# An attention and feed-forward kernel whose instruction order is written by a list scheduler in the kernel file, with a first chunk of 512 tokens

## The chip, the core and the metric

The kernel runs on one core of a Trainium2 chip. The metric is device time in microseconds (us) of one execution, as the median of several. A core has five engines, each with its own instruction queue: TensorE (PE in the profile; its weight loads are shown as PEld), VectorE (DVE), ScalarE (ACT), GpSimd (POOL) and SyncE (SP), which here issues all transfers. PSUM is the memory into which TensorE writes, in eight banks of 512 float32 columns on 128 partitions; everything else lies in SBUF.

## The reference

Inputs are q, k and v of shape 8 x 8 x 576 x 64 (batch, heads, positions, head width), and two weight matrices, 512 x 2048 and 2048 x 512. Two attentions are added and a feed-forward layer follows:

```python
    q_d = q.reshape(B, H, Sd, factor, D).mean(axis=3)     # factor 4: 144 pooled positions; k_d, v_d alike
    out_up = np.repeat(sm_attn(q_d, k_d, v_d), factor, axis=2)
    mask = np.abs(pos[:, None] - pos[None, :]) < factor   # local attention over 7 neighbours
    scores = np.where(mask, scale * np.matmul(q, k.transpose(0, 1, 3, 2)), -1000000000.0)
    ...
    x = (out_up + out_local).transpose(0, 2, 1, 3).reshape(B * S, H * D)    # 4608 tokens x 512
    h = x @ w_in                                          # 2048 wide
    g = np.where(h >= 1, h, np.where(h <= -1, 0.0, (h + 1) ** 2 / 4))
    return g @ w_out
```

## The kernel before, in words

**Attention** goes by pairs of heads: a batch has four pairs, so there are 32 pairs, n = 0 to 31. The function `attention(n, ...)` (L154) is a generator cut into pieces by `yield`. A pair loads q and k (transposed, 288 KB each), windows of v (320 KB) and pooled v (288 KB). DVE sums q and k in groups of four (L161, L165). PE computes local scores of ten windows of 64 positions into `sl_ps` (L186) and pooled scores into `sp_ps` (L200; a third of them goes to free columns of `sl_ps`). DVE and ACT, with help of POOL, make the two softmaxes (L218 to L260). For the pairs of batch 0 (`early`) the band mask is added by PE, with two matmuls of the identity with the band (L174), and POOL normalises (L254); for all others DVE adds the band (L221), POOL subtracts the maximum (L225), and DVE normalises. PE transposes both (`tl_ps` L272, `tp_ps` L284), ACT copies them out of PSUM, PE multiplies with v (`pl_ps` L306, `pp_ps` L318), and DVE adds the two (L329). The result x is split into a rounded part `xh` (ACT, L336) and a remainder `xl` (POOL, L337), in a ring buffer of two batches.

**Weights** come as 64-bit floating-point words, which the kernel converts itself, in 32 tiles (`convert_weights`, L354; tile f of w_in and of w_out for f = 0 to 15): two ACT operations on the halves of the words (L360, L362), a shift and an addition on DVE (L365, L366), then the split into a rounded part (ACT, L368) and a remainder (DVE, L369). All converted tiles stay in SBUF.

**The feed-forward layer** goes by chunks of 384 tokens, twelve chunks, and for each by 16 steps f of 128 hidden columns. `mm1` (L439) does twelve matmuls (four blocks of inputs, times hi x hi, lo x hi and hi x lo) into `h_ps`; then come ACT (L458, L459), DVE (L460), ACT for the rounded part `gh` (L463) and POOL for the remainder `gl` (L464). `mm2` (L467) does nine matmuls (three groups of 128 tokens, three products) and accumulates over the 16 steps in three banks `o_ps`; after the last step ACT copies them and SP stores them. Chunk 0 needs all tiles of weights for the first time, so the 32 conversions lie ahead of and in it, together with the attention of batch 1 (pairs 4 to 7).

**The order.** Up to the end of pair 3 and through chunk 0, the order in which work is emitted is written out by hand in two lists, `BEFORE_STEPS` and `FIRST_STEPS` (L76, L80): `q` and `v` are loads, `w` loads of weights, `a0` the next piece of pair 0, `c` a conversion, `s` a step of mm1, `m` one of mm2. From chunk 1 on a loop does at each step some pieces of attention, an `mm1`, and the `mm2` of an earlier step (L490). This order gives the priorities; the framework's scheduler makes each engine's instruction order from them, and `mm1`'s elementwise part is raised in priority (L455).

**PSUM.** In the first stage (pairs 0 to 3) there are `ps_a2` (2 banks), `ps_a1` (1 bank), `ps_b2` (2 buffers of 2 banks) and `ps_b1` (1 bank), used in rotation. Afterwards the b pools give way to `ps_h` (2 banks) and `ps_o` (3 banks), and all attention goes through `ps_a2` and `ps_a1`.

## Time and profile before

| what | value |
|---|---|
| median of 3 runs | 1008.16 us (1005.01 to 1008.43) |
| the profiled execution | 1007.57 us |
| its span, first to last instruction | 1005.8 us |
| instructions | 18468 |
| granted TensorE clock, mean | 0.98 of full speed |
| busy: PE / ACT / DVE / POOL | 969.0 / 488.6 / 396.3 / 351.2 us |

The span is a little shorter than the execution's time, since that also holds what lies before the first and after the last instruction. The profile's views that are used below are: the page's list of engines and its row of 40 equal slices (each digit is the busy share in tenths); the busy times of each engine in chosen windows; the timeline, with an instruction's start, its duration and, in brackets, how long its engine had been idle before it and what it waited for; and groups of equal instructions with their count, their total busy time and the mean duration of one in nanoseconds, and behind a bar the idle time ahead of them. An instruction's duration on PE is longer than the distance between two starts, because matmuls overlap; so PE's rates are read from starts.

### The profile page before, as it was taken

How to read it: one execution, taken by the hardware profiler on the slowest of the kernel's cores; microseconds unless marked ns; L12 is line 12 of the kernel's file. 1: busy time of each engine (PE TensorE's matmuls, PEld its weight loads, DVE VectorE, ACT ScalarE, POOL GpSimd, SP SyncE). 2: the span in 40 equal slices, each digit the busy share in tenths (PEclk: the TensorE clock that was granted, in tenths of full speed). 3: DMA queues.
4: the chain of work that ended last, by engine and by line, in shares of the span. 5: the costliest groups of instructions: out<-in, count | busy, mean ns of one | idle time of the engine just before them, and what ended most of it. 6: DMA issues, size and time to landing. Idle time of an engine off the chain costs nothing.

```text
span 1005.8 us, 18468 instructions
## 1 busy us (share of the span) xinstructions
PE 969.0 (96%) x7612; PEld 845.3 (84%) x7612; DVE 396.3 (39%) x700; ACT 488.6 (49%) x1063; POOL 351.2 (35%) x327
## 2 busy tenths in 40 slices
PE   5698999999999999999999999999999999999997
PEld 4476779998888888998888888999888888899996
DVE  6879991124434442113444434112434444111111
ACT  5778754335445444334445444434444454433433
POOL 2532443223434433223433334222334344222222
PEclk8689999999999999999999999999999999999999
DMA  9685111002112221002222112001212210000000
GB/s 304 228 294 172 50 50 57 1 12 92 50 50 94 61 74 57 1 1 66 64 74 71 59 50 75 33 1 41 63 50 74 91 63 15 32 1 1 32 1 33
DMA packets 26533, 66.24 MB, mean 66 GB/s; under 512 B 3152, under 2 KB 3152, under 8 KB 26448
## 3 DMA queue, kind: packets, MB, share of 16 engines
q1 hardware_dynamic: 26448, 65.06, 20.0%
q8 instruction: 60, 0.98, 0.4%
q14 instruction: 25, 0.20, 0.1%
HBM read 55.61 MB, written 9.44 MB: 65 GB/s over the span
## 4 chain that ended last, share of the span: by engine, by line
PE 79%; DVE 9%; issue 5%; POOL 3%; ACT 3%; DMA 1%; SPq 0%; POOLq 0%; DVEq 0%; ACTq 0%
PE h_ps L447 34%; PE o_ps L478 33%; PE tp_ps L284 2%; PE pl_ps L306 2%; PE sl_ps L186 2%; PE tl_ps L272 2%; DVE m L366 2%; PE pp_ps L318 2%; POOL gl L464 1%; PE sp_ps L200 1%; DVE m L365 1%; DVE w_o L369 1%; DMA raw_i<-w_in 1%; DVE w_i L369 1%; DVE u L460 1%
## 5 line engine op out<-in xcount | busy, mean ns | idle before, releaser
L447 PE MATMUL h_ps<-xh,w_i 128*128 128x384 f32 x1536 | 406.3, 344 | 0.6 <-DVE u L460 0.6
L464 POOL TENSOR_TENSOR gl<-u,gh 128x384 fp32r<-128x384 f32 x192 | 198.2, 1032 | 539.2 <-ACT gh L463 403.2
L478 PE MATMUL o_ps<-w_o,gh 128*128 128x512 f32 x1152 | 357.6, 391 | 1.0 <-ACT gh L463 1.0
L447 PEld LDWEIGHTS h_ps<-xh,w_i 128*128 128x128 f32 x1536 | 277.3, 188 | 20.9 <-issue 10.1
L460 DVE SCALAR_TENSOR_TENSOR u<-h_ps,u 128x384 f32<-128x384 f32 x192 | 106.8, 556 | 450.3 <-ACT u L459 424.3
L447 PE MATMUL h_ps<-xl,w_i 128*128 128x384 f32 x768 | 261.8, 341 | 0.0
L478 PEld LDWEIGHTS o_ps<-w_o,gh 128*128 128x128 f32 x1152 | 213.7, 188 | 33.4 <-ACT gh L463 1.7
L478 PE MATMUL o_ps<-w_o,gl 128*128 128x512 f32 x576 | 226.2, 393 | 3.8 <-POOL gl L464 3.6
L458 ACT ACTIVATE u<-h_ps 128x384 f32<-128x384 f32 x192 | 94.6, 492 | 272.8 <-PE h_ps L447 272.8
L463 ACT CAST gh<-u 128x384 fp32r<-128x384 f32 x192 | 98.6, 514 | 112.8 <-DVE u L460 112.8
L447 PEld LDWEIGHTS h_ps<-xl,w_i 128*128 128x128 f32 x768 | 144.4, 188 | 0.7 <-issue 0.4
L478 PEld LDWEIGHTS o_ps<-w_o,gl 128*128 128x128 f32 x576 | 108.1, 188 | 30.4 <-POOL gl L464 7.3
L459 ACT ACTIVATE u<-u 128x384 f32<-128x384 f32 x192 | 100.4, 523 | 5.0
L225 POOL TENSOR_TENSOR sl<-sl,mxl 128x640 f32<-128x640 f32 x28 | 35.8, 1280 | 52.7 <-DVE mxl L224 52.7
L264 POOL TENSOR_TENSOR vh<-vp_sb 72x512 f32<-72x512 f32 x32 | 42.3, 1322 | 29.7 <-DMA vp_sb<-vp 15.5
L337 POOL TENSOR_TENSOR xl<-x,xh 128x576 fp32r<-128x576 f32 x32 | 46.2, 1445 | 14.5 <-ACT xh L336 14.5
L329 DVE TENSOR_TENSOR x<-pl_ps,xd 128x576 f32<-128x576 f32 x32 | 24.2, 755 | 56.0 <-ACT xd L327 56.0
L221 DVE TENSOR_TENSOR sl<-sl_ps,band_sb 128x640 f32<-128x640 f32 x28 | 23.1, 823 | 40.8 <-PE sl_ps L200 40.8
L249 DVE TENSOR_REDUCE sp_ps<-sl 128x10 f32<-128x640 f32 x32 | 26.4, 825 | 28.2 <-ACT sp L240 28.2
L306 PEld LDWEIGHTS pl_ps<-al,v_sb 64*64 64x64 f32 x1280 | 23.8, 145 | 14.1 <-issue 9.9
L272 PE MATMUL tl_ps<-ident,sl 128*128 128x128 f32 x160 | 25.7, 296 | 9.8 <-POOL sl L254 5.3
L272 PEld LDWEIGHTS tl_ps<-ident,sl 128*128 128x128 f32 x160 | 20.0, 151 | 16.3 <-POOL sl L254 6.2
(67 smaller groups left out, 756.2 us busy)
## 6 DMA issues: line engine op xcount, KB each, us to landing
v_sb<-vw SPq DMA_DIRECT2D x32, 320.0 KB
vp_sb<-vp SPq DMA_DIRECT2D x32, 288.0 KB
out<-osb SPq DMA_DIRECT2D x36, 256.0 KB
raw_i<-w_in SPq DMA_DIRECT2D x16, 512.0 KB
raw_o<-w_out SPq DMA_DIRECT2D x16, 512.0 KB
q_sb<-qT SPq DMA_DIRECT2D x28, 288.0 KB
k_sb<-kT SPq DMA_DIRECT2D x28, 288.0 KB
first_i<-qT SPq DMA_DIRECT2D x4, 288.0 KB
```

The lines of the kernel that those rows point to most:

```text
L225: nc.gpsimd.tensor_tensor(slf, slf, ml_n, op=ALU.subtract)
L264: nc.gpsimd.tensor_tensor(vh, vpt[:, :, 0:2, :], vpt[:, :, 2:4, :], op=ALU.add)
L272: nc.tensor.transpose(tl_v[:, g * P : (g + 1) * P], sl[:, g].rearrange("p r c -> p (r c)"), ident)
L306: nc.tensor.matmul(pl_v[hs, o : o + OUT_LEN[i]], v[rs, 2 * g + h, :], al[rs, g, c0 : c0 + OUT_LEN[i]], start=True, stop=True,)
L337: nc.gpsimd.tensor_tensor(xl[:, p, r0 : r0 + S], x, xh[:, p, r0 : r0 + S], op=ALU.subtract)
L447: nc.tensor.matmul(h[:, :TCH], wi[:, wt, cc * P : (cc + 1) * P], xt[:, cc, ts], start=(n == 0), stop=(n == 3 * NCC - 1),)
L458: nc.scalar.activation(u, h[:, :TCH], AF.Relu, bias=0.5, scale=0.5)
L459: nc.scalar.activation(u, u, AF.Square)
L460: nc.vector.scalar_tensor_tensor(u, h[:, :TCH], 1.0, u, op0=ALU.max, op1=ALU.min)
L463: nc.scalar.copy(gh, u)
L464: nc.gpsimd.tensor_tensor(gl, u, gh, op=ALU.subtract)
L478: nc.tensor.matmul(o, gt[:, ts], wo[:, wt, :], start=f == 0 and n == 0, stop=f == NFC - 1 and n == 2)
```

## The change

The two hand-written lists, the loop over steps and the PSUM pools go. In their place every operation is described to a class `Plan`: its engine, its expected duration, the operations it needs, the buffers it uses, and a key, the time at which it is due. `Plan.run` walks through time: for every engine it looks for the operations whose inputs and buffers are there, takes the one with the lowest key among those that can start within 0.15 us of the first, and of all engines the one that starts first; it marks its buffers and its end, with 0.10 us from one engine to another and 0.25 us from PE, and with operations on DVE that are marked `shared` prolonged by 0.7 of their overlap with POOL. `Plan.emit` then emits the operations in that order, under a manual schedule, so that each engine's instruction order is the planned one; the framework still puts in the semaphores.

Beside that:

- Chunks are 512, 256 and then ten times 384 tokens. Chunk 0 accumulates in four banks (4 to 7), chunk 1 in two.
- PSUM is one tile of eight banks, given out by the plan. Batch 0 uses four pairs of banks for `sl`, `sp`, `tl`, `tp` and `pl`; batch 1 uses banks 0 and 1 for all of these, chunk 0 and 1 use 2 and 3 for `h`; from batch 2 on `sp` has bank 2 and shares the second bank of `sl`, as before. `pp` goes into free columns of `pl`'s banks.
- `early`, the band mask by PE and the subtraction on DVE, now holds for eight pairs instead of four. Normalising (L254) is on DVE for all pairs. Maxima and sums of the softmaxes are in SBUF instead of PSUM, `qd` has two buffers and `gl` two instead of three.
- Weight tiles, the first batch's q, k, v and the scratch of pairs 1 and 3 share 32 slots: weights from f = 4 on wait for slots that batch 0 has held.
- Loads are issued in the planned order on SP: q and k of the first four pairs, then their v, then weights, and later pairs 30 us ahead of their due time.

```diff
-TCH = 384
-NCH = NT // TCH
-NTT = TCH // P
 RING = 2 * S
...
+CHUNKS = [(0, 512), (512, 256)] + [(t, 384) for t in range(768, NT, 384)]
+NCH = len(CHUNKS)
...
-BEFORE_STEPS = """
-    q0 v a0 a0 w q1 a0 a0 a1 w a1 q2 a0 a1 c a0 a1 a2 w c a0 a2 q3 a1 c a2 a0 a1 a2 a0 c
-    a3 a1 a3 a2 c a3 a0 a1 a2 a3 c a1 a2 a3 a1 a2 a3 a2 a3 w a2 a3 a3 w a3
...
-FIRST_STEPS = """
...
+class Plan:
+
+
+    LATENCY = 0.10
+    PE_LATENCY = 0.25
+    DMA_RATE = 370e3
+    DMA_LATENCY = 2.0
+    WINDOW = 0.15
+    BACKLOG = 4.0
+
...
+    def run(self):
...
+        while len(done) < total:
+            best = None
+            for e in engines:
+                cands = []
+                for o in ready[e]:
+                    t = based.get(o.n)
+                    if t is None:
+                        t = based[o.n] = settle(o)
+                    ok = True
+                    for b in o.bufs:
+                        if b.units is None:
+                            got = pick(b)
+                            if got is None:
+                                ok = False
+                                break
+                            t = max(t, got[0] + self.LATENCY)
+                    if ok:
+                        if e == "SP":
+                            t = max(t, dma_free - self.BACKLOG)
+                        cands.append((max(t, free[e]), o))
+                if not cands:
+                    continue
+                t0 = min(c[0] for c in cands)
+                t, o = min((c for c in cands if c[0] <= t0 + self.WINDOW), key=lambda c: (c[1].key, c[1].n))
+                if best is None or t < best[0]:
+                    best = (t, o)
+            if best is None:
+                stuck = [(o.name, o.key) for e in engines for o in ready[e]]
+                raise RuntimeError(f"no work can go on: {stuck[:20]}")
+            t, o = best
...
+            o.start = t
+            if o.eng == "SP":
+                free["SP"] = t + 0.05
+                dma_free = max(dma_free, t + self.DMA_LATENCY) + o.nbytes / self.DMA_RATE
+                o.end = dma_free
+            else:
+                end = t + o.cost
+                if o.shared:
+                    for a, z in pool_busy[-4:]:
+                        end += max(0.0, min(end, z) - max(t, a)) * 0.7
+                if o.eng == "POOL":
+                    pool_busy.append((t, end))
+                free[o.eng] = o.end = end
+            ready[o.eng].remove(o)
...
+    def emit(self):
+        for o in self.done:
+            for b in o.bufs:
+                if b.tile is None:
+                    b.tile = b.make(b.units)
+            o.fn()
...
+    ps = ppool.tile([P, 8, 512], F32, name="ps")
...
+    def pe_step(c):
+        n = CHUNKS[c][1]
+        return 12 * {512: 0.227, 384: 0.177, 256: 0.122}[n] + n // P * 3 * 0.227
+
+    T0 = K["t0"]
+    pos = {}
+    t = T0
+    for c in range(NCH):
+        for f in range(NFC):
+            pos[c, f] = t
+            t += pe_step(c) if c else max(pe_step(c), K["conv"])
+    pos[NCH, 0] = t
+
+    def pair_key(n):
+        b = n // NPAIR
+        if b == 0:
+            return -100 + K["p0"] * n
+        if b == 1:
+            return pos[0, 0] + K["p1"] + K["p1d"] * (n - 4)
+        c = min(c for c in range(NCH) if CHUNKS[c][0] + CHUNKS[c][1] > S * b)
+        return pos[c - 1, 0] + K["p2"] + K["p2d"] * (n % NPAIR)
+
...
+        early = n < K["early"]
...
+        l_q = op("SP", 0, lambda: nc.sync.dma_start(qb.tile, qT[b, p]), bufs=[qb], key=k0 - ld, nbytes=295e3, name=name + "lq")
...
+        pairs_of_banks = [(0, 1), (2, 3), (4, 5), (6, 7)] if first else [(0, 1)]
+        slp = psum(pairs_of_banks)
...
+        o_sl = op("PE", 2.2 if first else 1.3 if early else 0.9, scores, [l_q, l_k, None if extra else before.get("tl")], [slp, qb, kb_], kk[1], name=name + "sl")
+        shares = b > 1
+        spp = psum([(2,)] if shares else pairs_of_banks)
...
+        o_sp = op("PE", 1.2 if first else 0.6, pooled, [o_qd, o_kd, None if extra else before.get("tp"), o_sl if shares else None],
+                  [spp, qdb, kdb] + [slp] * shares, kk[2], name=name + "sp")
...
+            o_s = op("DVE", 0.80, lambda: nc.vector.tensor_tensor(slf(), sl_n(), ml_n(), op=ALU.subtract),
+                     [o_m], [slp, mlb, slb], kk[2], name=name + "sub")
...
+        o_n = op("DVE", 0.82, lambda: nc.vector.tensor_tensor(
+            slf(), slf(), parts_b.tile[:, 0:NB].unsqueeze(2).broadcast_to([P, NB, WIN]), op=ALU.mult),
+            [o_r], [slb, parts_b], kk[4], name=name + "norm", shared=True)
...
+        plp = psum(pairs_of_banks)
...
+    def convert(kind, f):
+        op = plan.op
+        src = w_in if kind == "i" else w_out
+        kc = pos[0, f] - K["clead"] + (0 if kind == "i" else K["cio"])
+        wb = sbuf("w" + kind, None, None, "w", [range(8), range(8, 16), range(16, 24), SLOTS][(2 * f + (kind == "o")) // 8])
...
+        o4 = op("DVE", 0.70, lambda: nc.vector.tensor_tensor(mb.tile.bitcast(I32), mb.tile.bitcast(I32), rb.tile[:, :, 0], op=ALU.add),
+                [o2, o3], [rb, mb], kc, name=f"c4{kind}{f}", shared=True)
...
+        hb = psum([(2,), (3,)] if c < 2 else [(3,), (4,)])
...
+        o1 = op("PE", 12 * {512: 0.227, 384: 0.177, 256: 0.122}[n], run, xd + wd, [hb, wb], key, name=f"m1 {c},{f}")
...
+            o6 = op("POOL", 1.06 + e * 2.5, lambda: nc.gpsimd.tensor_tensor(glb.tile[:, :n], u(), ghb.tile[:, :n], op=ALU.subtract),
+                    [o5], [ub, ghb, glb], key, name=f"gl {c},{f}")
...
+                ob[c, t] = psum([(base + (t if c != 1 else 0) + j,) for j in (range(1) if c != 1 else range(4))] if c < 2 else [(5,), (6,), (7,)])
...
+    total = plan.run()
+    PLANNED.append((total, plan))
+    with tc.manual_schedule():
+        plan.emit()
...
+K = dict(t0=40.0, conv=6.5, p0=6.5, p1=7.7, p1d=18.0, p2=-15.0, p2d=14.0, early=8, dk=2.3, ld0=70.0, lv0=7.5, ld=30.0,
+         clead=10.0, cio=11.9, wld=-35.0, lead=9.1, xlv=0, glv=0)
```

765 lines of the change are left out of this document (427 added, 338 removed).

## The prediction

> **What bounds the kernel now.** I read the page first, for the engine that is full and where it is not.
>
> ```profile
> PE 969.0 (96%) x7612; PEld 845.3 (84%) x7612; DVE 396.3 (39%) x700; ACT 488.6 (49%) x1063; POOL 351.2 (35%) x327
> ...
> PE   5698999999999999999999999999999999999997
> ...
> DVE  6879991124434442113444434112434444111111
> ...
> PEclk8689999999999999999999999999999999999999
> ```
>
> TensorE (PE) is the engine that sets the end, and it is short of work only in the first six or so of the 40 slices (25 us each); VectorE (DVE) is nearly full in just those. Then I cut the span at three points: the first feed-forward matmul, the end of the first token chunk, and shortly before the end.
>
> ```profile
> 0.00:55.70 55.70, 35.57 (x480) 27.09 (x480) 40.26 (x68) 36.30 (x80) 22.03 (x24) 0.72 0.78 256
> 55.70:161.00 105.30, 94.88 (x789) 77.29 (x788) 92.65 (x148) 75.11 (x161) 42.03 (x33) 0.97 0.39 133
> 161.00:985.60 824.60, 823.40 (x6275) 728.29 (x6275) 261.75 (x482) 370.49 (x812) 283.11 (x266) 1.00 0.15 45
> ```
>
> The columns are PE, PEld, DVE, ACT, POOL busy, PE clock, DMA share, GB/s. After 161 us PE is busy 823.4 of 824.6 us: nothing of note is to be had there, except by doing fewer or cheaper matmuls, and the change does neither. Before it, 161 us pass. What PE needs is read off the starts of its instructions (start, duration, instruction, how many alike are merged into the row):
>
> ```profile
> 55.74 0.69 PE L447 MATMUL h_ps<-xh,w_i 128*128 128x384 f32 x1
> ...
> 160.48 0.52 PE L447 MATMUL h_ps<-xh,w_i 128*128 128x384 f32 x2
> ...
> 172.96 0.52 PE L447 MATMUL h_ps<-xh,w_i 128*128 128x384 f32 x2
> ...
> 175.08 0.62 PE L478 MATMUL o_ps<-w_o,gh 128*128 128x512 f32 x2
> ...
> 177.12 0.52 PE L447 MATMUL h_ps<-xh,w_i 128*128 128x384 f32 x2
> ...
> 254.20 0.71 PE L272 MATMUL tl_ps<-ident,sl 128*128 128x128 f32 x5
> ...
> 275.30 0.71 PE L272 MATMUL tl_ps<-ident,sl 128*128 128x128 f32 x5
> ...
> 1001.06 0.39 PE L478 MATMUL o_ps<-w_o,gl 128*128 128x512 f32 x1
> ```
>
> One step of 384 tokens is 177.12 - 172.96 = 4.16 us: twelve first-layer matmuls in 2.12 us (0.177 each) and nine second-layer ones in 2.04 (0.227 each). From one attention pair to the next, with four steps between, 275.30 - 254.20 = 21.10 us pass, so a pair costs PE 21.10 - 4 x 4.16 = 4.46 us. From 55.74 to the end PE needs 192 x 4.16 + 28 x 4.46 = 923.6 us, plus 4.3 from the last matmul's end (1001.45) to the end of the span, 927.9. It takes 1005.8 - 55.7 = 950.1. So 22 us are lost after 55.7. Chunk 0 (16 steps, 4 pairs, one step of chunk 1's first layer) needs 66.6 + 17.8 + 2.1 = 86.5 and takes 160.48 - 55.74 = 104.7: **18 us of the 22 are lost in chunk 0**, some 3 to 4 in all the rest. And 55.7 us go by before it starts.
>
> Why chunk 0 is slow, DVE's groups from 0 to 161 us say (count, then busy us and mean ns):
>
> ```profile
> L369 DVE TENSOR_TENSOR w_o<-m,w_o 128x512 fp32r<-128x512 f32 x16 | 16.2, 1013 | 0.9 <-ACT w_o L368 0.8
> L366 DVE CUSTOM_DVE_ANT_0 m<-raw_o,m 128x1024 uint16<-128x1024 uint16 x16 | 16.1, 1009 | 0.1
> L369 DVE TENSOR_TENSOR w_i<-m,w_i 128x512 fp32r<-128x512 f32 x16 | 13.8, 862 | 0.4 <-ACT w_i L368 0.2
> L365 DVE TENSOR_SCALAR m<-raw_o 128x512 int32<-128x512 int32 x16 | 13.0, 813 | 0.0
> L366 DVE CUSTOM_DVE_ANT_0 m<-raw_i,m 128x1024 uint16<-128x1024 uint16 x16 | 12.1, 759 | 0.1
> L460 DVE SCALAR_TENSOR_TENSOR u<-h_ps,u 128x384 f32<-128x384 f32 x17 | 9.3, 548 | 5.9 <-ACT u L459 5.8
> L365 DVE TENSOR_SCALAR m<-raw_i 128x512 int32<-128x512 int32 x16 | 7.5, 468 | 3.9 <-ACT raw_i L360 3.4 <-POOL gl L464 0.5
> ...
> L254 DVE TENSOR_TENSOR sl<-sl,sp_ps 128x640 f32<-128x640 f32 x4 | 3.2, 802 | 0.0
> ```
>
> Converting the 32 weight tiles costs DVE 16.2 + 16.1 + 13.8 + 13.0 + 12.1 + 7.5 = 78.7 us, 2.46 a tile. The first tile of all had it cheaper, 0.43 + 0.69 + 0.69 = 1.81 with overlap:
>
> ```profile
> 9.80 0.43 DVE L365 TENSOR_SCALAR m<-raw_i 128x512 int32<-128x512 int32 x1 [3.40 <-ACT raw_i L360]
> 10.37 0.69 DVE L366 CUSTOM_DVE_ANT_0 m<-raw_i,m 128x1024 uint16<-128x1024 uint16 x1
> ...
> 11.75 0.69 DVE L369 TENSOR_TENSOR w_i<-m,w_i 128x512 fp32r<-128x512 f32 x1 [0.24 <-ACT w_i L368]
> ```
>
> So 32 x (2.46 - 1.81) = 21 us are swelling beside POOL, which had little to do at 10 us. Of DVE's 132.9 us up to 161 (40.26 + 92.65) that is the larger part, and each step of chunk 0 needs two more tiles, whatever its number of tokens.
>
> **The change, part by part.** *Chunk 0 of 512 tokens instead of 384.* The same 32 conversions now lie under more matmuls. A step has 12 + 12 matmuls of 512 columns; taking L478's 0.227 for both kinds, 24 x 0.227 = 5.45 us, 16 steps 87.2, pairs 4 to 7 17.8. Those pairs now get the band by two matmuls each (the `early` branch, 8 pairs instead of 4); its row below, at the first stage's half clock, has 0.405 a piece, by columns at full clock 0.15, so 0.3 a pair, bounds 0.3 and 0.8, together 1.2. PE in chunk 0: 106.2 us.
>
> ```profile
> L174 PE MATMUL sl_ps<-band_r,ident_r 128*128 128x384 f32 (+1 forms) x8 | 2.5, 405 | 0.9 <-ACT sp L240 0.9
> ```
>
> For that DVE swaps an addition (0.82) for a subtraction (0.80) and POOL loses L225; the normalisation of pairs 0 to 3 goes from POOL to DVE. POOL's rows up to 161 us:
>
> ```profile
> L254 POOL TENSOR_TENSOR sl<-sl,sums 128x640 f32<-128x640 f32 x4 | 6.1, 1513 | 0.0
> L225 POOL TENSOR_TENSOR sl<-sl,mxl 128x640 f32<-128x640 f32 x4 | 5.5, 1385 | 11.9 <-DVE mxl L224 11.9
> ```
>
> DVE to the end of chunk 0: 132.9, plus 4 x 0.80 (L254's row) = 3.2, plus 16 clampings of 512 columns. Those have no row; L460's 548 ns scaled by columns gives 731 at most and 548 at least, so 0 to 2.9, I take 2.2 (part of an instruction is fixed). POOL is relieved of 11.6 of its 64 us (22.03 + 42.03), so of the swelling go at most 21 x 11.6 / 64 = 3.8, at least 0; I take 3.8, less POOL's longer gl. Together about 135 us, and DVE cannot start before q lands:
>
> ```profile
> 4.48 0.76 DVE L161 TENSOR_REDUCE qd<-first_i 128x144 f32<-128x576 f32 x1 [4.48 <-DMA first_i<-qT]
> ```
>
> So DVE alone would be through at 140, if never idle. PE's bound is start + 106. The two are close, so both will show: I add 3 us of stall to PE's (before: 18).
>
> *The start.* DVE worked 40.26 us in the first 55.7, and in that time six tiles were converted (6 x 2.46 = 14.8), three of w_in as here and three of w_out:
>
> ```profile
> L365 DVE TENSOR_SCALAR m<-raw_i 128x512 int32<-128x512 int32 x3 | 1.7, 553 | 3.4 <-ACT raw_i L360 3.4
> ```
>
> The plan orders conversions by the due time of their step, less 10 us, so about two tiles, 4.9 us, come before the start. 4.48 + 40.26 - 14.8 + 4.9 + 3.2 = 38.0 us for DVE; then the last pair's tail on PE, which took from the transpose at 49.63 to 55.74, 6.1 us:
>
> ```profile
> 22.62 1.33 PE L272 MATMUL tl_ps<-ident,sl 128*128 128x128 f32 x5 [2.56 <-POOL sl L254]
> ...
> 32.46 1.30 PE L272 MATMUL tl_ps<-ident,sl 128*128 128x128 f32 x5 [2.45 <-ACT sp L240]
> ...
> 47.62 1.23 PE L318 MATMUL pp_ps<-ap,vd 72*64 72x144 f32 x8 [2.08 <-DVE sums L253]
> 49.63 1.33 PE L272 MATMUL tl_ps<-ident,sl 128*128 128x128 f32 x5 [0.79 <-POOL sl L254]
> ```
>
> 38.0 + 6.1 = 44.1: **start at 44 us** (bounds: 40 if the tail lies under conversions, 55.7 if nothing is gained). The waits on POOL for L254 seen here go with the move to DVE. Eight PSUM banks I cost at nothing: the old pools are 2 + 1 + 2 x 2 + 1 = 8 banks in that stage too, only cut otherwise. Loads: all q and k first, then v, then weights; batch 0 is 8 x 288 + 4 x (288 + 320) KB = 4.7 MB, 13 us at the rate seen here, so the last pair's data is there long before DVE comes to it. Weight loads from tile pair 4 on wait on SP until scratch of batch 0 is free, and hold what stands behind them; 16.8 MB at that rate are 45 us, over by 60 to 75, while the last tile is due after 120. Row of that rate:
>
> ```profile
> 10.00:20.00 10.00, 7.09 (x153) 5.71 (x152) 9.60 (x18) 7.94 (x18) 1.16 (x1) 0.87 1.03 370
> ```
>
> *Chunk 1 of 256 tokens.* Its first-layer matmul has no row. By columns, 0.177 - (0.227 - 0.177) = 0.127; if something fixed holds it, 0.177. I take 0.127, since 384 and 512 differ by just the columns. Step: 12 x 0.127 + 6 x 0.227 = 2.89, 16 steps 46.2 us (at 0.177, 55.8). Clamping, squaring and splitting must fit into 2.89 us a step: the largest is POOL's gl, 1.03 us for 384 columns, so they do, and two gl buffers instead of three are enough with a step of 4.16 us.
>
> ```profile
> L464 POOL TENSOR_TENSOR gl<-u,gh 128x384 fp32r<-128x384 f32 x192 | 198.2, 1032 | 539.2 <-ACT gh L463 403.2
> ...
> L447 PEld LDWEIGHTS h_ps<-xh,w_i 128*128 128x128 f32 x1536 | 277.3, 188 | 20.9 <-issue 10.1
> ```
>
> [...]
>
> *Ten chunks of 384, the order written by the planner.* 160 x 4.16 = 665.6, pairs 8 to 31 24 x 4.46 = 107.0, loss 2.7 (as before after 160.48), tail 4.3. Pooled scores and maxima now go through other buffers at the same counts: nothing on PE. On SP the stores and loads stand in the planned order; at 45 GB/s after 161 us a late one is covered by a whole step.
>
> **Sum:** start 44 + chunk 0 106.2 + stall 3 + 46.2 + 665.6 + 107.0 + 2.7 + 4.3 = 979.0 us of span. The profiled execution had 1007.57 us for 1005.8 of span, so 1.8 more: 980.8. Its time is 0.6 below the median 1008.16, so I say **981**.
>
> **Rivals.** *A, the first stage stays as long:* DVE shares with POOL and the conversions swell as in the rows above (468 against 813 ns in L365's two rows). Batch 1 also runs sl, sp, tl, tp and pl one after another through bank pair 0 and 1, so sp now waits until DVE has done with sl, and a late DVE holds each of the five in turn, with chunk 1 behind them. Start 50, stall 11: 981 + 6 + 8 = 995. For it: DVE is at 92.65 of 105.3. Against: PE's bound for chunk 0 grows from 86.5 to 106.2.
>
> *B, chunk 1 bound by the weight loads:* 0.177, + 9.6 = 991. The weight loads' row has 188 ns each, more than 127, which speaks for it; that 188 fits under 177 already, against it.
>
> *C, slower than before: the written order stalls PE in every pair.* Where an attention matmul stands in PE's queue ahead of ready feed-forward work and its input is late, all behind it waits. Before had such, in chunk 0:
>
> ```profile
> 97.81 0.71 PE L318 MATMUL pp_ps<-ap,vd 72*64 72x144 f32 x8 [1.67 <-DVE sp L258]
> ...
> 112.89 0.80 PE L306 MATMUL pl_ps<-al,v_sb 64*64 64x61 f32 x40 [0.97 <-ACT sp L240]
> ```
>
> A pair has six such entries. With two stalls of 1.3 us in each of 24 pairs, 62 us: 1043; it decides from (1008 - 981) / 24 = 1.1 us a pair on. Against: the plan puts PE's pair at 4.2 us where it takes 4.46, so the other engines are rather ahead; and first-layer work is due 9.1 us ahead, some 3 us more than 2.1 for its matmuls and 4 for the chain behind them. [...]
>
> *D, no change:* the planner's gain of about 27 us is eaten by stalls of 1 us a pair: 1006.
>
> **Chances.** Forecast (966 to 988) 0.55; A 0.18; B 0.06; C 0.15 in all its sizes; D 0.06. The measurement tells about 0.5%, 5 us, from no change. Faster: forecast, A, B and a little of D, 0.81; same 0.05; slower 0.14. The forecast's own range is 966 to 988: start at 40, no stall and no loss give 981 - 4 - 3 - 3 = 971, and some 5 less if PE's clock, 0.72 in the first stage, is full there. To hold 8 in 10 it must take in A and B: 966 to 1000.
>
> **What would show it.** First h_ps matmul near 44 us and six conversions no longer ahead of it; second chunk's first matmul near 153; PE busy in all windows after; 128x256 matmuls about 127 ns apart; DVE busy nearly throughout 5 to 145. I am wrong if PE has idle time behind attention matmuls in windows after 200 us, or if chunk 0 takes more than 115 us from its start.

## The result and the profile after

The changed kernel takes **990.89 us** (median of four runs, 990.36 to 991.99), the kernel before 1008.24 beside it (1005.01 to 1008.43): a ratio of 0.9837, 95% interval 0.9815 to 0.9859. That is faster, by some 17 us, and 10 us short of the 981 that was forecast. It lies inside the wide range of 966 to 1000, but outside the forecast's own range of 966 to 988, between it and rival A's 995. The profiled execution took 991.34 us, with a span of 989.3.

First the page of the changed kernel, its list of engines and two of its rows of 40 slices:

```profile
PE 964.3 (97%) x7620; PEld 835.6 (84%) x7620; DVE 431.8 (44%) x704; ACT 487.4 (49%) x1063; POOL 340.1 (34%) x320
...
PE   6699999999999999999999999999999999999998
...
DVE  7799994135644441135444461114454543111110
```

TensorE (PE) is short of work in the first two slices only (a slice is 24.7 us). Before, its row began 5, 6, 9, 8, so it was short within the first four, not in "the first six or so", as the prediction reads it; it was VectorE (DVE) that was nearly full in the first six. DVE is busy 35 us more than before. The forecast had some 2 us more up to the end of chunk 0 (135 for 132.9) and named nothing after it; where the rest comes from is told with the last experiment. The span cut at the start of the feed-forward, at the start of chunk 1, and shortly before the end shows the same (columns as in the prediction: PE, PEld, DVE, ACT, POOL, PE clock, DMA share, GB/s):

```profile
0.00:50.00 50.00, 31.42 (x515) 25.14 (x515) 39.51 (x63) 25.80 (x63) 16.31 (x21) 0.77 0.95 320
50.00:158.97 108.97, 107.34 (x782) 84.41 (x783) 104.26 (x156) 89.31 (x173) 39.31 (x28) 0.98 0.32 112
158.97:966.00 807.03, 805.96 (x6232) 709.23 (x6231) 285.77 (x483) 364.46 (x814) 280.35 (x267) 1.00 0.14 46
```

In chunk 0 PE is busy 107.34 of 108.97 us, and DVE 104.26. After it PE lacks 1.07 us in 807. The stages' bounds are read off PE's timeline (start, duration, instruction, and in brackets the idle time ahead of it and what it waited for):

```profile
49.99 1.22 PE L647 MATMUL ps<-xh,w_i 128*128 128x512 f32 x2 [0.55 <-DVE x L563]
...
53.57 0.63 PE L647 MATMUL ps<-xl,w_i 128*128 128x512 f32 x1
...
61.34 0.62 PE L687 MATMUL ps<-w_o,gh 128*128 128x512 f32 x2
...
66.93 0.62 PE L647 MATMUL ps<-xh,w_i 128*128 128x512 f32 x2
...
158.97 0.40 PE L647 MATMUL ps<-xh,w_i 128*128 128x256 f32 x2
...
161.80 0.62 PE L687 MATMUL ps<-w_o,gh 128*128 128x512 f32 x2
...
164.59 0.40 PE L647 MATMUL ps<-xh,w_i 128*128 128x256 f32 x2
```

Chunk 1's first layer starts at 158.97, and 2.79 us of chunk 0's second layer (161.80 to 164.59) still follow. So against the terms of the forecast:

| stage | forecast | measured | miss |
|---|---|---|---|
| start of the feed-forward | 44 | 49.99 | +6.0 |
| chunk 0, with its stalls | 106.2 + 3 = 109.2 | 158.97 - 49.99 + 2.79 = 111.8 | +2.6 |
| the rest | 46.2 + 665.6 + 107.0 + 2.7 + 4.3 = 825.8 | 989.3 - 161.76 = 827.5 | +1.7 |

The misses sum to 10.3, which is 989.3 less the forecast span of 979.0. More than half is the start.

**The hole in the first stage.** Four rows, one of each engine's timeline (SPq is the queue of DMA issues):

```profile
17.19 1.77 SPq L604 DMA_DIRECT2D raw_i<-w_in  x2
...
27.66 0.67 ACT L608 ACTIVATE raw_i<-raw_i 128x512 f32<-128x512 f32 x1 [8.82 <-DMA raw_i<-w_in]
...
30.42 0.76 DVE L563 TENSOR_TENSOR x<-ps,xd 128x576 f32<-128x576 f32 x1 [5.15 <-ACT xd L555]
...
31.23 1.50 PE L504 MATMUL ps<-ident,sp 128*72 128x128 f32 x6 [8.47 <-DVE x L563]
```

From 18.84 to 27.66 us ScalarE (ACT) stands before the first conversion of a weight tile, L608, and waits for the tile. Behind it in ACT's order are the second tile's conversion, the exponential of a pair's scores and the copy `xd`; DVE needs the last two and stops for 5.15 us, and PE needs DVE and stops for 8.47. The tile's load was issued at 17.19, behind the q, k, vp (pooled v) and v of the first pairs, and landed 10 us later. The plan had it there sooner, because it counts 370 kB per us (`DMA_RATE`), and the rates in the windows of 5 us (last column) are:

```profile
5.00:10.00 5.00, 5.00 (x114) 4.08 (x114) 4.42 (x8) 0.63 (x1) 0.00 (x0) 1.00 1.04 378
10.00:15.00 5.00, 2.34 (x48) 1.77 (x47) 4.91 (x9) 1.86 (x8) 2.45 (x2) 0.86 1.01 273
15.00:20.00 5.00, 4.47 (x107) 3.65 (x108) 4.90 (x11) 2.58 (x9) 1.99 (x2) 0.80 0.91 242
20.00:25.00 5.00, 1.08 (x11) 0.57 (x7) 4.93 (x7) 0.00 (x0) 3.21 (x3) 0.88 1.05 321
25.00:30.00 5.00, 0.00 (x0) 0.00 (x0) 0.27 (x1) 2.27 (x4) 0.95 (x2) 0.50 1.02 392
```

The DMA engines are full in all five windows (share 0.91 to 1.05). They move 378 GB/s while mostly q and k come (batch 0 has 2.4 MB of them, and 2.7 MB are moved by 10 us), and 392 when weights come; but from 10 to 25 us, when mostly v and pooled v come, only 242 to 321. A plan that believes 370 throughout puts ACT's conversion too early in the order, and ACT kept to the written order when it ran: DVE had done the exponential's scores at 21.94 us, and the exponential ran at 29.49, after the first tile's conversion. That was the theory to test.

### The profile page after: what moved, and what is told of

It is laid out like the page before. It is cut to its first block, busy times and chain, and to the rows that moved or that the text cites. A ratio compares the mean times of both kernels' runs of the same rounds, so it can differ in the third digit from the quotient of the medians.

```text
span 989.3 us, 18499 instructions
## 1 busy us (share of the span) xinstructions
PE 964.3 (97%) x7620; PEld 835.6 (84%) x7620; DVE 431.8 (44%) x704; ACT 487.4 (49%) x1063; POOL 340.1 (34%) x320
## 4 chain that ended last, share of the span: by engine, by line
PE 88%; DVE 7%; DMA 3%; ACT 2%; issue 1%; SPq 0%; ACTq 0%; DVEq 0%
PE ps L687 39%; PE ps L647 38%; PE ps L370 2%; PE ps L527 2%; PE ps L504 2%; PE ps L488 2%; PE ps L545 2%; PE ps L395 2%; DMA vp<-vp 1%; DMA raw_i<-w_in 1%; DVE m L615 1%; ACT sp L450 1%; DVE mxp L445 1%; DVE sl L469 1%; DVE sums L460 1%
## 5 line engine op out<-in xcount | busy, mean ns | idle before, releaser
L647 PE MATMUL ps<-xh,w_i 128*128 128x384 f32 (+2 forms) x1536 | 395.8, 340 | 0.6 <-DVE x L563 0.6
L668 POOL TENSOR_TENSOR gl<-u,gh 128x384 fp32r<-128x384 f32 (+2 forms) x192 | 197.2, 1027 | 523.8 <-ACT gh L663 373.7
L687 PE MATMUL ps<-w_o,gh 128*128 128x512 f32 x1152 | 368.8, 401 | 0.0
L647 PEld LDWEIGHTS ps<-xh,w_i 128*128 128x128 f32 x1536 | 277.1, 189 | 22.7 <-issue 4.2
L661 DVE SCALAR_TENSOR_TENSOR u<-ps,u 128x384 f32<-128x384 f32 (+2 forms) x192 | 106.3, 554 | 434.3 <-ACT u L660 427.3
L647 PE MATMUL ps<-xl,w_i 128*128 128x384 f32 (+2 forms) x768 | 259.6, 338 | 0.0
L687 PEld LDWEIGHTS ps<-w_o,gh 128*128 128x128 f32 x1152 | 207.3, 188 | 40.2 <-issue 6.9
L687 PE MATMUL ps<-w_o,gl 128*128 128x512 f32 x576 | 226.5, 393 | 0.0
L663 ACT CAST gh<-u 128x384 fp32r<-128x384 f32 (+2 forms) x192 | 98.5, 513 | 107.0 <-DVE u L661 100.1
L647 PEld LDWEIGHTS ps<-xl,w_i 128*128 128x128 f32 x768 | 144.6, 188 | 3.0
L687 PEld LDWEIGHTS ps<-w_o,gl 128*128 128x128 f32 x576 | 108.1, 188 | 25.3
L582 POOL TENSOR_TENSOR xl<-x,xh 128x576 fp32r<-128x576 f32 x32 | 46.3, 1446 | 24.2 <-ACT xh L577 15.7
L563 DVE TENSOR_TENSOR x<-ps,xd 128x576 f32<-128x576 f32 x32 | 24.2, 756 | 35.6 <-ACT xd L555 34.7
L527 PEld LDWEIGHTS ps<-al,v 64*64 64x64 f32 x1280 | 22.9, 139 | 9.8 <-issue 4.9
```

Of the source, the lines that this page charges most:

```text
L527: nc.tensor.matmul(pl_v[hs, o : o + OUT_LEN[i]], vb.tile[rs, 2 * g + h, :], alb.tile[rs, g, c0 : c0 + OUT_LEN[i]], start=True, stop=True,)
L582: o_xl = op("POOL", 1.445, lambda: nc.gpsimd.tensor_tensor(xl[:, p, r0 : r0 + S], xb.tile, xh[:, p, r0 : r0 + S], op=ALU.subtract), [o_xh] ...
L647: nc.tensor.matmul(h, wi[:, wt, cc * P : (cc + 1) * P], xt[:, cc, ts], start=(i == 0), stop=(i == 3 * NCC - 1))
L661: o4 = op("DVE", 0.556 + e * 1.2, lambda: nc.vector.scalar_tensor_tensor(u(), h(), 1.0, u(), op0=ALU.max, op1=ALU.min), [o3], [hb, ub], ke ...
L663: o5 = op("ACT", 0.51 + e, lambda: nc.scalar.copy(ghb.tile[:, :n], u()), [o4], [ub, ghb], key, name=f"gh {c},{f}")
L668: o6 = op("POOL", 1.06 + e * 2.5, lambda: nc.gpsimd.tensor_tensor(glb.tile[:, :n], u(), ghb.tile[:, :n], op=ALU.subtract), [o5], [ub, ghb, ...
```

## Experiments

The theory: ACT's in-order wait for a weight tile that the plan believes landed makes the hole, and the hole is most of the miss. The rivals: the start is bound by DVE's or PE's own work whatever the loads do; the parts of the change that were costed at nothing are not nothing; the order counts for less than the chunks' sizes.

**Loads of the first tile of each matrix ahead of v.** The order of each engine is kept; only two DMA issues move on SP. i0 and o0 are the first tiles of w_in and w_out.

```diff
     total = plan.run()
+    first_w = [o for o in plan.done if o.name in ("lwi0", "lwo0")]
+    rest = [o for o in plan.done if o.name not in ("lwi0", "lwo0")]
+    at = [o.name for o in rest].index("a3lk") + 1
+    plan.done = rest[:at] + first_w + rest[at:]
```

> Only the two loads of weight tiles 0 are moved, to behind q and k of pair 3 and ahead of all v; every other instruction keeps its place. Theory (in the changed kernel ACT waits 8.8 us, from 18.8 to 27.7 us, for the first weight tile, and all attention work queued behind it waits too): ACT's long wait goes, first feed-forward matmul near 43 us instead of 50.0, time 991 - 6 = 985 us (982 to 987). Rival (the transfers are full in the first 50 us, 0.95 of all engines, so whatever comes first makes another late): v comes 3 us later, PE waits for it instead, start 48 to 50 us, time 989 to 992.

Measured: 992.03 us (990.41 to 994.18), ratio 0.9855 [0.9832, 0.9878]; span 990.0, start of chunk 0 at 51.34. No gain, against the expectation. ACT's timeline says why:

```profile
30.41 0.65 ACT L608 ACTIVATE raw_i<-raw_i 128x512 f32<-128x512 f32 x1 [9.28 <-DMA raw_i<-w_in]
```

i0 was converted at 19.89 us without a wait, but next in ACT's order stands tile i1 of w_in, not o0, and i1's load had not been moved. The hole is the same, one instruction later, and v, now behind two tiles of weights, came late to POOL, for which ACT then waited 3.11 us at 17.70. The edit moved the wrong pair of loads; it does not speak against the theory.

**Loads of i0 and i1 moved.** The same edit with the two tiles that ACT's order has first, put behind the v of the second pair:

```diff
+    first_w = [o for o in plan.done if o.name in ("lwi0", "lwi1")]
+    rest = [o for o in plan.done if o.name not in ("lwi0", "lwi1")]
+    at = [o.name for o in rest].index("a1lv") + 1
```

> ACT converts tile 0 of w_in, then tile 1 of w_in, both ahead of the attention of pairs 1 to 3; the first experiment had moved the load of tile 1 not at all, and ACT waited for that one until 30.4 us. Now the loads of these two tiles go to behind v of pair 1, all else in the changed kernel's order. Theory (one in-order wait of ACT, 8.8 us long, sets the start): no ACT wait over 3 us for w_in, start 43 to 47 us, time 984 to 987 us. Rival (the first 50 us are full of transfers, so what is moved ahead makes v of pairs 2 and 3 as late): start 49 us or later, 989 to 992.

Measured: 987.54 us (986.01 to 989.29), ratio 0.9814 [0.9793, 0.9835]; span 985.4. What is left on ACT and PE:

```profile
30.74 0.65 ACT L608 ACTIVATE raw_o<-raw_o 128x512 f32<-128x512 f32 x1 [3.92 <-DMA raw_o<-w_out]
...
34.83 1.33 PE L527 MATMUL ps<-al,v 64*64 64x61 f32 x40 [4.88 <-ACT al L494]
...
46.17 1.22 PE L647 MATMUL ps<-xh,w_i 128*128 128x512 f32 x2
```

The wait for w_in is gone, one of 3.92 us for w_out has come, and the start is at 46.17 instead of 49.99. The span is 3.9 us shorter, the start 3.8. From the start to chunk 1's first matmul it is 108.93 us here and 108.98 in the changed kernel, and from there to the end 830.3 in both: what is won at the start arrives at the end. With no computing engine's order changed and no work taken out, this shows the wait to be the cause of that part of the miss. The medians differ by 3.4 us; the ratios to the kernel before, taken on different chips, by only 0.0023 (2.3 us), and their intervals overlap, so the size is less sure than the direction.

**The plan's transfer rate 270 instead of 370.** Here the loads stay and the plan learns when they land.

```diff
-    DMA_RATE = 370e3
+    DMA_RATE = 270e3
```

> The planner's transfer rate is 270 instead of 370 kB per us, nearer to the 242 to 321 GB/s of the changed kernel between 10 and 25 us; all orders are planned anew with it. Theory (the hole comes from a planned landing of the first weight tile that was some 8 us too early): the first conversion is put later in ACT's order, the hole goes, start 43 to 46 us, time 983 to 987 us. Rival (the late tile itself sets the start, wherever its conversion stands): start at 49 us or later, time 989 to 992.

Measured: **985.53 us** (984.59 to 986.88), ratio 0.979 [0.9769, 0.9811]; span 985.1, start 46.35. This is less than either kernel's time. The windows:

```profile
10.00:20.00 10.00, 6.21 (x139) 4.95 (x143) 9.84 (x18) 5.09 (x16) 4.35 (x5) 0.83 0.98 257
20.00:30.00 10.00, 5.56 (x83) 4.01 (x80) 9.83 (x16) 4.92 (x13) 5.73 (x5) 0.83 1.00 361
30.00:40.00 10.00, 7.17 (x75) 5.31 (x76) 9.86 (x15) 7.42 (x18) 3.71 (x3) 0.61 0.52 193
```

ACT waits for no tile of w_in, and DVE is now full: 9.83 to 9.86 in each 10 us. That is the picture the forecast had assumed, and the start is still 2.35 us behind its 44; where those lie is told below.

**Rates of 310 and 240, and the changed kernel again**, all on one chip, to see whether the time follows the rate or an order merely happened to be good.

> The changed kernel once more, unaltered, so that the two runs beside it are compared on one chip. Theory (the hole in the first stage is in the program's order, not a chance of one execution): 989 to 992 us, ScalarE again waits 8 to 10 us for a tile of w_in near 22 to 28 us, start of chunk 0 at 48 to 52 us. Rival (the profiled execution was an unlucky one): no such wait, start under 47 us, time 985 to 987.

> The planner assumes 310 kB/us for every transfer instead of 370. Some 6.44 MB stand ahead of the first w_in tile in the queue, so the plan has it landed at about 21 + 3 = 24 us (17.4 + 3 in the change as it is), where it really lands at 27 to 28. Theory (the hole is the difference between the planned and the real landing): a wait for w_in of 3 to 5 us is left on ScalarE, start 47 to 49 us, 987 to 990 us, between the change (991) and the rate of 270 (985.5). Rival (any other rate only reshuffles the order, by chance for better or worse): no ordering by rate; the wait is as long as with 370 or gone altogether.

> The planner assumes 240 kB/us. Planned landing of the first w_in tile 6.44 MB / 240 + 3 = 29.8 us, later than the real one. Theory: no wait for w_in, start 45 to 48 us, 984 to 988 us, the same as with 270 within 2 us. Rival (reshuffling): a time over 989 or under 983 us.

| rate in the plan | time, us | ratio to before | ACT's wait for w_in | start | start to chunk 1 | chunk 1 to the end | span |
|---|---|---|---|---|---|---|---|
| 370 (unaltered) | 990.93 (988.93 to 991.38) | 0.9841 [0.9821, 0.9862] | 4.91 | 47.31 | 108.98 | 830.5 | 986.8 |
| 310 | 989.43 (987.96 to 990.79) | 0.9827 [0.9807, 0.9846] | 5.52 | 47.83 | 110.36 | 830.2 | 988.4 |
| 270 (another chip) | 985.53 (984.59 to 986.88) | 0.979 [0.9769, 0.9811] | none | 46.35 | 109.98 | 828.8 | 985.1 |
| 240 | 988.71 (988.57 to 988.81) | 0.9823 [0.9804, 0.9842] | none | 45.04 | 111.37 | 830.2 | 986.6 |

The columns from the wait on are of the profiled execution; the wait is the idle time ahead of L608 in ACT's timeline, the start the first L647 in PE's.

The control repeats the time, but its profiled execution is its quickest (988.93), and there the wait is 4.91 us instead of the 8.82 of the first profile. The tile landed at 25.21 instead of 27.66 us, the start came 2.7 us sooner and the span is 2.5 us shorter, the program being the same. So the expectation of 8 to 10 us was too narrow; the hole's depth varies from one execution to the next, with the landing of the loads. The wait is there with 370 and 310 and gone with 270 and 240, as the theory has it, and the profiled start moves from 47.3 to 50.0 down to 45.0. Between 370 and 310 the times differ by less than their intervals, though, the wait and the start of the two profiled executions even lie the other way round, and 240 comes out at 988.71 where 984 to 988 was expected. After chunk 1 has begun, the same work is left in both:

```profile
156.33:985.10 828.77, 823.10 (x6325) 726.65 (x6323) 287.79 (x486) 372.54 (x829) 284.93 (x271) 1.00 0.15 46
```

```profile
156.41:986.60 830.19, 824.39 (x6325) 727.13 (x6323) 288.03 (x486) 372.25 (x829) 284.66 (x271) 1.00 0.15 46
```

These are the windows from chunk 1's first matmul to the end, first with 270, then with 240: all but equal counts on every engine, 1.4 us apart. And the start that 240 has 1.3 us sooner is lost again within chunk 0 (111.4 us against 110.0). So it is shown that the wait is gone in the plans with 270 and 240; that 270 is better than 240 by the order itself isn't: of the 1.5 us between the two spans, 1.4 are a longer time for the same instructions, and the two ran on different chips.

**Twelve chunks of 384**, everything else as changed:

```diff
-CHUNKS = [(0, 512), (512, 256)] + [(t, 384) for t in range(768, NT, 384)]
+CHUNKS = [(t, 384) for t in range(0, NT, 384)]
```

> The planner as it is, but twelve chunks of 384 tokens. Theory (chunk 0 is bound by DVE's conversions, and 512 tokens put more matmuls under them): start 50 us, chunk 0 takes 100 to 106 us as before the change, and then 11 x 66.6 + 24 x 4.46 + 7 us follow: 50 + 103 + 847 = 1000 us of span, 1002 us (998 to 1006), so of the 17 us gained some 11 hang on the chunk. Rival (the planned order alone removed the stalls): chunk 0 takes 88 to 92 us, time 988 to 992.

Measured: 1003.62 us (1002.54 to 1005.54), ratio 0.9966 [0.9954, 0.9979]; span 1002.0, start 49.54. Chunk 0 with one step of chunk 1's first layer takes 105.0 us (the next step begins at 154.55), where it took 104.7 before the change. Within it PE's waits come back. From the view of waits (what waited for what: total us, times, the longest):

```profile
PE ps L647 <- DVE w_i L623: 3.8, 3, 1.9
PE ps L488 <- DVE sl L469: 2.7, 1, 2.7
```

In the changed kernel's own chunk 0 no wait for a converted tile is left, and PE's longest wait is 0.99 us. With 384 tokens PE is busy 93.2 of the 105.5 us from 49.54 to 155 and DVE 97.7. So DVE bounds chunk 0, as before the change, and all of the change but its chunks brings 1006.75 (the kernel before on this chip) less 1003.62 = 3.1 us. The other 12.7 us (1003.62 - 990.89) hang on the chunks of 512 and 256.

**Six banks instead of eight in the first batch:**

```diff
-        pairs_of_banks = [(0, 1), (2, 3), (4, 5), (6, 7)] if first else [(0, 1)]
+        pairs_of_banks = [(0, 1), (2, 3), (4, 5)] if first else [(0, 1)]
```

> Batch 0 has three pairs of PSUM banks instead of four (six banks). Theory (the banks are no limit in the first stage; transfers and queues are): start between 48 and 52 us, time 988 to 994 us. Rival (the eighth bank lets pairs overlap): start 54 us or later, time 995 us or more.

Measured: 991.63 us (990.96 to 995.16), ratio 0.9857 [0.9833, 0.9882], the same within the interval. Its profiled execution is its longest: 995.16 with the start at 54.49, the rival's figures, but with 11.15 us of ACT's wait for w_in; the other runs lie at 991 to 992, as the theory has it. In the median the fourth pair of banks is worth nothing that can be measured.

**The first batch's normalisation back on POOL**, together with the rate of 270, so that the hole doesn't cover it:

```diff
-        o_n = op("DVE", 0.82, lambda: nc.vector.tensor_tensor(
+        vs = nc.gpsimd if first else nc.vector
+        o_n = op("POOL" if first else "DVE", 1.3 if first else 0.82, lambda: vs.tensor_tensor(
```

> The version with the planner's rate at 270, and in batch 0 POOL normalises the local softmax instead of DVE, as before the change. Theory (once the hole is gone DVE sets the start, 4 x 0.8 us less for it): start 44 to 46 us instead of 46.4, time 982 to 986. Rival (POOL's 1.5 us operations swell DVE's and lengthen each pair's chain): start 47 us or later, 986 to 990.

Measured: 991.09 us (990.49 to 991.65), ratio 0.9849 [0.9831, 0.9867], 5.6 us more than with the rate alone. The start is as early (46.11), but it is 112.64 us from there to chunk 1 instead of 109.98. In PE's timeline:

```profile
34.88 1.30 PE L488 MATMUL ps<-ident,sl 128*128 128x128 f32 x5 [1.24 <-POOL sl L469]
...
43.80 0.90 PE L358 MATMUL ps<-band_r,ident_r 128*128 128x384 f32 x2 [2.50 <-DVE x L563]
...
138.82 0.74 PE L488 MATMUL ps<-ident,sl 128*128 128x128 f32 x5 [1.70 <-DVE sl L469]
```

PE waits for POOL again (1.24 us), then longer for DVE. Giving this work to POOL wins nothing at the start and costs 2.7 us in chunk 0. The profiled spans are 4.0 us apart (989.1 and 985.1); another 1.6 of that come after chunk 1 has begun, where the edit changes no operation, so the whole 5.6 us can't be put down to the move.

**Conversions due 5 us ahead instead of 10** (`clead=5.0`), with the rate of 270:

> The version with the planner's rate at 270, and conversions due 5 us instead of 10 us ahead of their step. Theory (DVE is full up to the start and four tiles are shifted ahead of it): one or two tiles fewer before the start, start 43 to 45 us, but DVE is then late in chunk 0 by about as much: time 983 to 987, the same within 2 us. Rival (conversions are not DVE's limit in chunk 0): the whole 2 to 3 us are won, 982 to 983.

Measured: 986.96 us (986.77 to 987.56), ratio 0.9809 [0.9791, 0.9827]; span 984.8, start 44.91. The start is 1.4 us sooner, and chunk 0 gives 1.2 of it back (111.14 us to chunk 1 instead of 109.98): PE waits 2.1 us for converted tiles, twice, where with the rate alone it waited 1.3, once. When a conversion is done sets which of the two stages waits, not how much DVE has to do.

**The band mask by PE for four pairs instead of eight** (`early=4`), otherwise as changed:

> The changed kernel with the band mask of pairs 4 to 7 added by DVE and the maximum subtracted by POOL, as before the change (4 x 2 matmuls fewer, 4 x 1.39 us more on POOL). By the prediction's sum PE saves 1.2 us and POOL's load costs DVE up to 2 us: chunk 0 the same within 3 us, time 988 to 994. Rival (the mask by PE matters, since the pairs' chain in banks 0 and 1 is the limit): chunk 0 longer by 4 us or more, 995 us.

Measured: 991.69 us (990.56 to 992.62), ratio 0.9855 [0.9835, 0.9874]: the same as the changed kernel within the interval. The band's matmuls for pairs 4 to 7 neither cost nor bring anything that can be measured.

**Maxima and sums back in PSUM.** DVE's 35 us more than before lie in four groups, which gain 39 us while others lose a little. One of them, over the whole run, of the kernel before and of the changed one:

```profile
L238 DVE TENSOR_SCALAR mxp<-sp_ps 128x3 f32<-128x3 f32 x32 | 4.8, 150 | 0.0
```

```profile
L445 DVE TENSOR_SCALAR mxp<-mx 128x3 f32<-128x3 f32 x32 | 26.1, 816 | 1.1
```

The same scaling of three numbers per partition, 150 ns from PSUM and 816 from SBUF: 21.3 us more. Likewise the sums' addition of 1e-9 (5.6 to 12.1 us), the pooled normalisation (20.9 to 27.3) and L469 (22.9 to 27.6, of which 3.2 is the work moved from POOL). The change had moved these small tiles from PSUM to SBUF. The last run puts them back into free columns of the pair's `sp` bank, with the rate of 270:

```diff
-        sums_w = sbuf("sums", [P, NB + NQB], F32, "sums", [0, 1])
-        parts_b = sbuf("parts", [P, NB + NQB], F32, "parts", [0, 1])
-        mx2 = sbuf("mx2", [P, NQB], F32, "mx2", [0, 1])
+        def mx2():
+            return spp.tile[:, 0, 2 * SD : 2 * SD + NQB]
+
+        def sums():
+            return spp.tile[:, 0, 2 * SD + 4 : 2 * SD + 4 + NB + NQB]
```

> On top of the rate of 270: the pooled maxima, the sums and the reciprocals of the softmaxes lie in free PSUM columns of the pair's sp bank, as in the kernel before, instead of SBUF; nothing else. Theory (DVE instructions whose operands are all in SBUF stand still while POOL runs, those with one in PSUM do not): the mean of mxp (128x3) goes from 0.17 to 0.42 us in the changed plan to 0.15, that of adding 1e-9 to the sums from 0.82 and 0.44 to 0.17, of the two normalisations from 1.1 and 1.40 to 0.82 and 0.60 in the first batch. With rate 270 that is 4 x (0.65 + 0.27 + 0.80) = 6.9 us of DVE in the first stage and some 4 in chunk 0. DVE was full there, so the start comes 3 to 6 us sooner, at 40 to 43 us, and the time is 979 to 983. Rival 1 (the swelling comes of DVE's and POOL's load at large, wherever operands lie): the means stay, 985 to 987. Rival 2 (the swelling goes, but the first stage is set by chains between engines or by the sp bank being held longer): the means fall, the start stays at 44 to 47, 984 to 988.

Measured: 987.74 us (987.39 to 989.98), ratio 0.9823 [0.9805, 0.9842]; span 985.6, start 45.23. DVE's groups up to 50 us, first with the rate of 270 alone, then with the tiles in PSUM:

```profile
L472 DVE TENSOR_TENSOR sp<-sp,parts 128x432 f32<-128x432 f32 x4 | 5.6, 1401 | 0.0
L469 DVE TENSOR_TENSOR sl<-sl,parts 128x640 f32<-128x640 f32 x4 | 4.3, 1087 | 0.1
L464 DVE TENSOR_SCALAR sums<-sums 128x13 f32<-128x13 f32 x4 | 3.3, 819 | 0.0
```

```profile
L471 DVE TENSOR_TENSOR sl<-sl,ps 128x640 f32<-128x640 f32 x4 | 3.3, 822 | 0.1
...
L474 DVE TENSOR_TENSOR sp<-sp,ps 128x432 f32<-128x432 f32 x4 | 2.4, 596 | 0.0
...
L466 DVE TENSOR_SCALAR ps<-ps 128x13 f32<-128x13 f32 x4 | 0.7, 180 | 1.6 <-ACT sp L452 1.4
```

The swelling of these groups is gone, to the expected values, and DVE's busy time in the whole run falls from 430.3 to 404.5 us. The time does not fall: rival 2. The start is 1.1 us sooner, not 3 to 6. Up to 159 us the conversions, whose operands stay in SBUF, take 79.4 us instead of 73.0, so DVE's load up to there falls by only 1.1 (142.65 to 141.57). Whether the conversions swell because the small instructions no longer stand in the way isn't shown: they take 73.0 to 81.0 us in the runs here, and the plan was made anew. And DVE now waits for ACT's exponentials (L452, 1.4 us in the row above). After 159 us, where most of the 26 us are saved, PE sets the end. A saving on DVE that doesn't show: true of the place, without worth for the time.

## Why the prediction was right in sign and 10 us short

**The step that failed: "start at 44 us".** The sum was 4.48 us until q lands and 33.6 of DVE's work (together the 38.0), then a tail of 6.1 from the last pair's transposition on PE to the start. Two things in it were wrong. First, DVE was taken to have something to do all the time. It stood still for 5.15 us behind ACT: the prediction looked at the weights' landing only for the late tiles and for SP, with 370 GB/s from a window of before; for the first tiles it asked when DVE would want them, and not what stands behind the wait on ACT. Second, the tail is 3.7 us longer, and it stays long when the hole is gone:

| | last pair's transposition | tail | start |
|---|---|---|---|
| forecast | 38.0 | 6.1 | 44.1 |
| before | 49.63 | 6.11 | 55.74 |
| changed | 40.15 | 9.84 | 49.99 |
| loads of i0 and i1 moved | 36.09 | 10.08 | 46.17 |
| rate 270 | 35.98 | 10.37 | 46.35 |
| rate 240 | 34.71 | 10.33 | 45.04 |

The forecast took the tail from the row of before, where PE was busy 6.11 of the 6.11 us and DVE 2.48. In the changed kernel PE is busy 6.13 of the 9.84 us and DVE 9.81: conversions that the sum had put ahead of the tail, or behind the start, lie in it. DVE's work up to the start is 39.5 us where 33.6 were summed; 9.4 of it are conversions, where two tiles, 4.9 us, were counted. Rows of the tail, by time:

```profile
41.87 1.90 DVE L623 TENSOR_TENSOR w_i<-m,w_i 128x512 fp32r<-128x512 f32 x1
43.69 1.21 DVE L615 CUSTOM_DVE_ANT_0 m<-raw_i,m 128x1024 uint16<-128x1024 uint16 x1
44.93 0.62 ACT L620 CAST w_i<-m 128x512 fp32r<-128x512 f32 x1 [1.56 <-DVE m L615]
46.02 0.63 ACT L512 COPY ap<-ps 72x576 f32<-72x576 f32 x1
46.69 0.71 PE L545 MATMUL ps<-ap,vd 72*64 72x144 f32 x8 [2.65 <-ACT ap L512]
```

The last pair's copy `ap` stands in ACT's order behind the rounding of a converted tile, L620, which waits for DVE: as in the hole, but shorter (1.56 us of ACT, 2.65 of PE, where the hole had 8.82 and 8.47). Take the hole away and the transposition comes at 34.7 to 36.1, sooner than 38.0, while the tail keeps its 10 us (9.0 in the last experiment); so the start stays 1 to 2.4 us late. That the conversions make the tail long is read off these rows; no run took them out of it (due 5 us later, they still left it 10.36).

Rival A gave "start 50, stall 11" and 995. The start of 50 came true, in part for A's cause (the conversions in the tail swell, 1.90 and 1.21 us where the prediction's first tile had 0.69; POOL runs L582 from 41.54 to 43.21 and L480 from 43.18 to 44.35), in part for the hole, which A did not name; the stall of 11 did not come.

**Chunk 0: 106.2 + 3 became 111.8.** PE's idle time is under the 3 us allowed: 108.97 - 107.34 = 1.6. The rest is PE slower than its price. The first matmuls run at half the clock: the granted clock is 0.50 in each us from 48 to 54, 0.74 in the next and 1.00 from 55 on. From 49.99 to 54.70 there are 11 matmuls, 4.71 us where 11 x 0.227 = 2.5 were priced: 2.2 us are lost. What lowers the clock and brings it back isn't shown: PE's long pause ahead of this was 2.65 us (44.04 to 46.69), the full clock came some 4.5 us after the steady matmuls began, and from 35 to 40 us the clock stayed at 0.50 though PE was busy for the whole 5 us. After 54.70 the matmuls of 512 columns are 0.2305 us apart in the first layer and 0.232 in the second, in the groups of three with no attention beside them, where 0.227 was taken: 181 x 0.0035 + 192 x 0.005 = 1.6 us. With the smaller stall, 1.6 for 3, that gives 2.2 + 1.6 - 1.4 = 2.4, near the 2.6 measured.

**DVE in chunk 0.** DVE was busy 39.51 + 104.26 = 143.8 us up to 158.97; the forecast was 135 to the end of chunk 0. The clampings were right to the nanosecond (2.2 us over the old ones gives 685 for one, and one takes 685), which is luck, since 2.2 was picked from 0 to 2.9. The fixed part that the choice supposed is there: in the changed kernel a clamping of 256 columns takes 425 ns, of 384 553 and of 512 685, some 130 for each 128 columns, which leaves some 165, an estimate from these three. The relief was not right:

```profile
L615 DVE CUSTOM_DVE_ANT_0 m<-raw_i,m 128x1024 uint16<-128x1024 uint16 x16 | 19.0, 1186 | 0.7 <-ACT raw_i L610 0.2
L623 DVE TENSOR_TENSOR w_i<-m,w_i 128x512 fp32r<-128x512 f32 x16 | 15.5, 970 | 0.0
L615 DVE CUSTOM_DVE_ANT_0 m<-raw_o,m 128x1024 uint16<-128x1024 uint16 x16 | 12.9, 808 | 0.8 <-ACT raw_o L610 0.3
L623 DVE TENSOR_TENSOR w_o<-m,w_o 128x512 fp32r<-128x512 f32 x16 | 12.3, 769 | 0.0
L661 DVE SCALAR_TENSOR_TENSOR u<-ps,u 128x512 f32<-128x512 f32 x16 | 11.0, 685 | 2.3 <-ACT u L660 2.2
...
L469 DVE TENSOR_TENSOR sl<-sl,parts 128x640 f32<-128x640 f32 x8 | 7.4, 920 | 0.3
```

These are DVE's groups from 0 to 159 us. The conversions, these four groups and L613's 17.4 us, cost 77.1 us where they had cost 78.7, so "3.8 us less swelling" was 1.6; and L469, priced at 0.80, takes 0.92. The other part is a step that was costed at nothing, "pooled scores and maxima now go through other buffers at the same counts: nothing on PE". That is true of PE; on DVE their place has a price, as the last experiment shows: up to the end of chunk 0 the scaling of the maxima goes from 1.2 to 4.1 us, the addition to the sums from 1.3 to 2.4, and the pooled normalisation from 6.7 to 7.3. The error stayed small in the time because PE, not DVE, sets chunk 0's length now.

**The rest: +1.7.** Chunk 1's matmuls of 256 columns are closer than forecast: 24 from 158.97 to 161.80, 0.118 each, not 0.127, and so 192 x 0.009 = 1.7 us shorter. The other terms together are then 3.4 us too short. PE's idle time doesn't explain that (1.07 us from 158.97 to 966, of 2.7 allowed): it is longer work. After 165 us, in groups of three with no attention beside them, second-layer matmuls start 0.231 us apart (385 groups) where the kernel before has 0.227 (447), and first-layer ones of 384 columns 0.175, against 0.177 in the sum. A step of 384 tokens is then 12 x 0.1748 + 9 x 0.2309 = 4.18 us, not 4.16: 2.5 us more in 160 steps. What is left for the 24 pairs, once all feed-forward matmuls and the idle time are taken off, is 110 us, 4.58 a pair instead of 4.46: 2.8 us more. Why the second layer is slower isn't known; with the rate of 270 it is 0.228.

**Rivals.** B, chunk 1 bound by weight loads at 0.177, is refuted by the same 0.118. C, the written order stalling PE in every pair, and D, no change by 1 us a pair, are refuted by the 1.07 us. But the mechanism of C, an in-order engine standing before an operation whose input is late with ready work behind it, did happen, on ACT in the first stage: in the hole (8.82 us), and once more in the tail (1.56 us).

**What was costed at nothing.** The eight banks held (991.63 with six). The band for pairs 4 to 7, costed at 1.2 us of PE, showed neither cost nor gain without it; the row behind that price was not all at half clock, since in the kernel before the granted clock is 1.00 from 10 to 16 us and 0.50 from 18 to 26, and the eight matmuls, begun between 11.3 and 28.0 us, last from 274 to 686 ns. The move of L254's work to DVE, costed at 3.2 us against waits on POOL, was right in sign; undoing it with the hole gone costs 5.6 us, of which 2.7 are seen in chunk 0. The core of the forecast, that chunk 0 is bound by the conversions on DVE and more tokens over the same 32 tiles hide them, held: without the new chunks 12.7 us of the gain are gone. Neither of the signs of being wrong came: chunk 0 took less than 115 us from its start, and PE has no idle time worth naming after 200 us.

## What to carry to other kernels

A planner's written order is only as good as its durations, the transfers' too: take the rate from the stage in which the plan uses it (here 242 to 321 GB/s while v and pooled v come, not the 378 and 392 of q, k and the weights), and rather too low than too high, since here 240 and 270 cost nothing that could be measured, and 370 stopped ACT for 8.82 us with everything behind it in its order. When a start is forecast from an engine's busy time, list for each operation in that stretch which load it needs, when that lands, and what stands behind the wait; and before taking a stretch's length from the kernel before, ask which engine was busy in it and what the new order puts there. Before moving a load in an experiment, read in the consumer's order which one it waits for next; one run here was lost on that.
